# A convolution stem's backward pass: input gradient on plane differences, whose planes are turned to be the weight gradient's operands

## The chip, the cores and the metric

The kernel runs on one core of a Trainium2 chip. Its engines are TensorE (PE, matrix products into PSUM; PEld is its loading of weights), VectorE (DVE), ScalarE (ACT), GpSimd (POOL) and SyncE (SP, which here issues nearly all DMA transfers). Each runs its own list of instructions in order, and they wait for one another by semaphores. The metric is the device time of one execution in microseconds; lower is better.

## The reference

The forward pass is a convolution over time with 31 taps and stride 2, a normalisation over time of each batch and channel, and a GELU. The kernel returns the forward result and the four gradients.

```python
B, T, D, K = 2, 16000, 256, 31          # x [B,T,D], w [K,D,D], bf16
s = 2
L = (T - K) // s + 1                    # 7985
h = sum(einsum('blc,cd->bld', x[:, i:i + s * L:s, :], w[i]) for i in range(K))
mu, var = mean and variance of h over l
h = (h - mu) / sqrt(var + 1e-5) * gn_gamma + gn_beta
out_0 = gelu(h)
out_1, out_2, out_3, out_4 = gradients of x, w, gn_gamma, gn_beta for grad_out
```

## The kernel before

**The arithmetic.** A convolution by 31 taps is cut by the residue of time into sub-convolutions, and two of them are computed with three products instead of four (sums of data planes against differences of weights, or the other way round). This is done twice, which gives nine combinations of a branch `br` and a leaf `lf`, each one of A, B_, C_; the leaf B_ is shared, and its product is added to those of A and C_ as a "seed". Where a third such split is made, a leaf's 16 matmuls of G (`g_leaf`) become 4 (`g_outer`, or `g_three_b` for leaf B_) plus 8 (`g_three_ac`), and the seed has one more term. In the kernel before, leaf B_ is split everywhere, leaf A in the second batch (the set `GO`), and leaf C_ nowhere in G (`GOC` is empty).

**Stages.** F0 and F1 are the forward convolution of the two batches, each in four chunks (`forward`, `f_sums` for the sums of planes on DVE, `f_mm` L596 for the matmuls, `f_seed`); the GELU and its derivative of batch 0 (`gelu_batch`, `gelu_unit`, L954 to L980, one channel half `dh` of 1024 columns at a time) run on ACT and DVE beside F1. G0 and G1 are the input gradient (`input_grad`): for each batch, chunk `c`, half `pr` and branch, matmuls through `g_mm` (L1162). Its data are the planes of the gradient at h, which `e_load` and `e_comp` make from stored tensors and which `g_sums` (L1121) adds up: `first` for the branches, `second` for leaves A and C_, `third` for the further split. `g_seed` (L676 to L687) puts the shared product into the PSUM banks of A and C_, with `g_three_b`'s, `g_outer`'s and leaf B_'s kept results (`GRB`); `g_evac` (L691) takes finished banks out. The GELU of batch 1 runs beside G0. W is the weight gradient (`weight_grad`, matmuls at L1447): nine combinations n, each with sums of x (`w_add` L1413, `pair_x` L1508) and differences of the gradient at h (`leaf_d` L1587, `pair_d` L1516).

**What joins G and W.** W needs time on the partitions, so the gradient at h is turned by DMA (`dn_turn`: two turns of 512 KB and two stores for each chunk) and stored in time order in `dn_d`. `d2_piece` reads it back in seven pieces for each batch, subtracts on DVE (L1357) and stores the operands of eight of the nine combinations in `d2_d`; `d_tile` loads them in W. G itself works on sums of planes with differences of weights, so that none of its own planes is an operand of W.

**Order.** A recording class `Plan` holds every operation with its duration, and orders them by due times: those of PE from their place in the list, the others backwards from who needs them, shifted by a table `lead` for each kind of operation and stage. Per engine, the written order is the order of issue. SP has one list for all loads, stores and turns; a turn is `dma_start_transpose` (L420), another transfer L415. PSUM is four tiles `ring` of two banks; a branch takes two (`px`, `pt`), and two branches are in work at once.

Of the kernel before, what the change touches and what calls it, by code (L numbers as in the profile page):

```python
# [10 lines left out]
FP32 = mybir.dt.float32  # L11
# [27 lines left out]
class Plan:  # L39
# [3 lines left out]
    def __init__(self, tc):  # L43
# [10 lines left out]
            "F0 f_mm f_three_ac": -2.5,  # L54
            "F0 f_mm f_three_b": -4.0,
            "F0 f_mm pe_turn": 9.5,
            "F0 f_three_b f_first": 2.0,
            "F0 f_three_b forward": 2.5,
            "F0 keep f_first": 4.5,
            "F0 load load_w": -4.5,  # L60
            "F0 put x_first": -4.5,
            "F0 tt second": -1.0,
            "F0 tt third": -1.5,
            "F0 turn w2_part": 8.0,
            "F0 turn x_load": -3.5,
            "F0 ve f_first": -1.0,
            "F0 ve f_seed": -4.0,
            "F0 w_sub f_first": 2.0,
            "F1 f_mm f_leaf": -4.0,
            "F1 f_mm f_three_ac": -3.0,  # L70
            "F1 f_mm f_three_b": -9.5,
            "F1 f_three_b forward": 4.5,
            "F1 gelu_unit gelu_batch": 3.0,
            "F1 load gelu_unit": -2.0,
            "F1 tiny elem_finalize": 2.0,
            "F1 tiny fwd_stats": -11.5,
            "F1 tt f_sums": 1.5,
            "F1 tt gelu_unit": -4.0,
            "F1 tt second": -7.5,
            "F1 turn x_load": -3.0,  # L80
            "G0 e_comp conv_stem_kernel": -1.0,
            "G0 g_mm g_three_ac": 3.0,
            "G0 g_mm g_three_b": -3.0,
            "G0 g_three_b input_grad": 6.0,
            "G0 keep g_evac": -3.0,
            "G0 load dn_turn": 1.0,
            "G0 load e_load": 4.5,
            "G0 load gelu_unit": 2.0,
            "G0 load load_w2": 4.0,
            "G0 tiny elem_finalize": -8.5,  # L90
            "G0 tt first": -2.0,
            "G0 tt second": -9.0,
            "G0 turn gelu_batch": -7.0,
            "G0 w_sub load_w2": -8.0,
            "G1 e_comp conv_stem_kernel": 12.5,
            "G1 g_mm g_leaf": -4.0,
            "G1 g_mm g_outer": -1.5,
            "G1 g_mm g_three_ac": -4.0,
            "G1 keep g_evac": -10.5,
            "G1 load dn_turn": -11.5,  # L100
            "G1 load e_load": -2.5,
            "G1 load g_evac": 20.0,
            "G1 signed g_seed": -7.5,
            "G1 spread e_comp": -5.5,
            "G1 sub d2_piece": -7.5,
            "G1 tt first": 9.5,
            "G1 tt second": -5.5,
            "G1 tt third": -2.0,
            "G1 ve_neg g_seed": 11.5,
            "W keep w_keep": -2.0,  # L110
            "W keep weight_grad": 3.0,
            "W leaf_d weight_grad": -2.0,
            "W pair_x weight_grad": -1.5,
            "W turn out0_late": -7.0,
            "W ve w_done": 12.0,
            "W ve weight_grad": -3.5,
            "W w_add weight_grad": -2.0,
            "W w_add x_tile": 3.0,
            "W w_both weight_grad": 9.0,
            "W w_emit w_done": 7.5,  # L120
            "W w_mm w_leaf": -3.5,
            "W w_mm w_single": 0.5,
            "W w_pairs weight_grad": -2.5,
        }
        self.room, self.mixed = 2048.0, 2.2
        self.overlap = {"DVE": 0.084, "ACT": 0.1}
        self.npe = 0
        self.stage = "F0"

# [205 lines left out]
def conv_stem_kernel(  # L335
# [217 lines left out]
    def i_tap(q, par, br, lf):  # L553
        return 8 * q + par + 4 * (lf == C_) + 2 * (br == C_)
# [1204 lines left out]
```

## Time and profile before

| | |
|---|---|
| runs | 1185.14, 1185.56, 1185.71 us; median 1185.56 |
| span of the profiled execution (the page has no other time of it) | 1187.8 us |
| forward matmuls (L596), first and last start | 4.7 and 428.8 us |
| matmuls of the input gradient (L1162) | 416.3 and 861.0 us |
| matmuls of the weight gradient (L1447) | 861.2 and 1183.5 us |
| DMA traffic | 255.17 MB in 334100 packets |

A group of instructions is shown as line, engine, operation, out<-in and shapes, count, then busy time and the mean duration of one, then the idle time of the engine just before them and who ended it. Matmuls overlap in the pipeline, so that their mean duration is a latency; what one costs is the busy time of the group divided by its count. Some matmul records are missing from a trace; weight loads tell the true count, one for each matmul. The rows themselves stand in the prediction.

### The profile page before, as it was taken

What the parts mean: (1) busy time and instruction counts of PE and PEld (TensorE: products, weight loads), DVE (VectorE), ACT (ScalarE), POOL (GpSimd) and SP (SyncE); (2) the same over time, 40 slices, a digit from 0 to 9 for tenths busy, and PEclk for the clock granted to TensorE, in tenths of its full rate; (3) what the DMA queues carried; (4) which work ended last, traced back from release to release, by engine and by line L of the source; (5) the groups of instructions that cost most, each with busy time, mean ns of one, the idle gap of its engine ahead of it and who ended that gap; (6) DMA issues with size and microseconds to landing.
All of it is one profiled execution on the core that took longest, in us unless ns stands there. A gap on an engine that the chain in (4) does not pass through costs nothing.

```text
span 1187.8 us, 19338 instructions
## 1 busy us (share of the span) xinstructions
PE 1149.0 (97%) x7739; PEld 763.5 (64%) x7796; DVE 1047.6 (88%) x1358; ACT 570.0 (48%) x873; POOL 18.9 (2%) x67
## 2 busy tenths in 40 slices
PE   5999999999999999999999999999999999989998
PEld 3888889777777964444444444444488656656685
DVE  7997898799999989999879997788889898777995
ACT  1254454788885578978884476433322212111200
POOL 0000000000000000000000000000000000000000
PEclk9999999999999999999999999999999999999999
DMA  9446949968986799567639998697998824986774
GB/s 212 73 115 122 200 121 182 205 146 204 204 209 124 270 353 252 167 225 186 221 115 292 270 329 265 161 318 266 317 235 266 271 90 151 359 300 198 239 219 140
DMA packets 334100, 255.17 MB, mean 215 GB/s; under 512 B 187500, under 2 KB 312682, under 8 KB 325738
## 3 DMA queue, kind: packets, MB, share of 16 engines
q1 hardware_dynamic: 333818, 253.93, 76.6%
q8 instruction: 61, 1.00, 0.3%
q14 instruction: 29, 0.24, 0.1%
q0 software_dynamic: 192, 0.00, 0.0%
HBM read 118.95 MB, written 89.62 MB: 176 GB/s over the span
## 4 chain that ended last, share of the span: by engine, by line
PE 46%; DVE 14%; DMA 6%; issue 4%; ACT 1%; SPq 0%; DVEq 0%; ACTq 0%
PE ps L1162 27%; PE ps L1447 15%; PE ps L596 4%; DVE arena L1413 3%; DMA arena<-in_x_dram 2%; DMA arena<-dnd 2%; DVE arena L1357 2%; DVE arena L1587 2%; DVE ps L676 1%; DVE arena L676 1%; DVE arena L1516 1%; DVE arena L1508 1%; DMA dnd<-arena 1%; DVE arena L1121 1%; DVE ps L1540 1%
## 5 line engine op out<-in xcount | busy, mean ns | idle before, releaser
L1162 PE MATMUL ps<-arena 128*128 128x512 bf16 x1974 | 429.7, 376 | 6.6 <-DVE ps L676 3.6
L596 PE MATMUL ps<-arena 128*128 128x256 bf16 (+4 forms) x3460 | 408.2, 281 | 17.8 <-DVE arena L551 7.1
L596 PEld LDWEIGHTS <-arena 128*128 128x128 bf16 x3460 | 338.1, 99 | 87.7 <-DVE arena L551 7.5
L1162 PEld LDWEIGHTS <-arena 128*128 128x128 bf16 x2016 | 197.3, 98 | 237.7 <-issue 6.8
L1447 PE MATMUL ps<-arena 128*128 128x256 bf16 (+1 forms) x2305 | 312.1, 298 | 10.5 <-DVE arena L1508 7.3
L1447 PEld LDWEIGHTS <-arena 128*128 128x128 bf16 x2320 | 228.1, 98 | 94.6 <-DVE arena L1508 8.7
L691 ACT ACTIVATE arena<-ps 128x1024 f32<-128x1024 f32 (+1 forms) x143 | 145.7, 1020 | 285.3 <-PE ps L1447 98.1
L561 DVE TENSOR_TENSOR arena<-arena 128x1087 bf16<-128x1087 bf16 (+3 forms) x211 | 175.5, 866 | 13.7 <-PE ps L596 12.4
L968 DVE TENSOR_TENSOR arena<-arena 128x1024 bf16<-128x1024 bf16 x160 | 107.0, 683 | 8.5 <-ACT arena L962 3.9
L1413 DVE TENSOR_TENSOR arena<-arena 128x4096 bf16<-128x4096 bf16 x38 | 86.3, 2284 | 20.8 <-DMA arena<-in_x_dram 19.5
L1121 DVE TENSOR_TENSOR arena<-arena 128x516 bf16<-128x516 bf16 (+3 forms) x176 | 83.6, 506 | 8.6 <-PE ps L1162 8.0
L676 DVE TENSOR_TENSOR ps<-ps,arena 128x1024 f32<-128x1024 f32 x60 | 73.1, 1224 | 7.9 <-PE ps L1447 4.5
L1357 DVE TENSOR_TENSOR arena<-arena 128x768 bf16<-128x768 bf16 (+3 forms) x112 | 65.4, 636 | 9.9 <-DMA arena<-dnd 4.7
L711 ACT ACTIVATE arena<-ps 128x512 bf16<-128x512 f32 (+1 forms) x64 | 36.9, 578 | 70.4 <-PE ps L596 67.9
L676 DVE TENSOR_TENSOR ps<-arena,ps 128x1024 f32<-128x1024 f32 x44 | 53.8, 1223 | 9.3 <-PE ps L1162 5.5
L1532 ACT COPY ps<-ps 128x256 f32<-128x256 f32 x54 | 19.3, 357 | 78.7 <-PE ps L1447 77.6
L1587 DVE TENSOR_TENSOR arena<-arena 128x2304 bf16<-128x2304 bf16 x36 | 47.4, 1348 | 4.8 <-PE ps L1447 4.8
L1516 DVE TENSOR_TENSOR arena<-arena 128x1024 bf16<-128x1024 bf16 x76 | 48.7, 682 | 1.6 <-DMA arena<-d2d 1.6
L551 DVE TENSOR_TENSOR arena<-arena 128x2048 bf16<-128x2048 bf16 (+1 forms) x52 | 49.8, 989 | 0.0
L958 DVE SCALAR_TENSOR_TENSOR arena<-arena 128x1024 bf16<-128x1024 bf16 x32 | 39.0, 1219 | 11.3 <-ACT arena L956 11.1
L1189 ACT ACTIVATE ps<-ps 128x512 f32<-128x512 f32 x48 | 27.9, 582 | 41.1 <-PE ps L1162 38.0
L1508 DVE TENSOR_TENSOR arena<-arena 128x2048 bf16<-128x2048 bf16 x38 | 45.3, 1216 | 1.2 <-PE ps L1162 1.2
(79 smaller groups left out, 632.8 us busy)
## 6 DMA issues: line engine op xcount, KB each, us to landing
arena<-in_x_dram SPq DMA_DIRECT2D x40, 1024.0 KB, 9.8
arena<-d2d SPq DMA_DIRECT2D x16, 1216.0 KB, 11.5
out_dram<-arena SPq DMA_DIRECT2D x14, 1024.0 KB, 4.4
d2d<-arena SPq DMA_DIRECT2D x30, 384.0 KB, 7.1
arena<-dnd SPq DMA_DIRECT2D x10, 960.0 KB, 5.8
vl<-arena SPq DMA_DIRECT2D x36, 256.0 KB, 3.3
arena<-vl SPq DMA_DIRECT2D x9, 1024.0 KB, 6.8
hd<-arena SPq DMA_DIRECT2D x8, 1024.0 KB, 5.0
```

Source lines behind the costliest of these rows:

```text
L561: lambda: nc.vector.tensor_tensor(out=o, in0=a, in1=b, op=ALU.add))
L596: yield nc.tensor.matmul(ps[:, dh, cs], lhsT=wt, rhs=mv, start=s0, stop=False, skip_group_check=True)
L676: add("DVE", dve(1024, 1), [out], [a, b], lambda: nc.vector.tensor_tensor(out=out, in0=a, in1=b, op=op))
L691: lambda: nc.scalar.activation(out=out, in_=ps, func=ACT.Copy, scale=scale))
L968: add("DVE", dve(1024), [o], [a, b_], lambda: V.tensor_tensor(out=o, in0=a, in1=b_, op=op))
L1121: lambda: nc.vector.tensor_tensor(out=o, in0=a, in1=b, op=ALU.add))
L1162: yield nc.tensor.matmul(ps[:, e, 0:wide], lhsT=lt, rhs=mv, start=s0, stop=False, skip_group_check=True)
L1357: lambda: nc.vector.tensor_tensor(out=out, in0=a, in1=b_, op=ALU.subtract))
L1413: add("DVE", dve(4096), [o], [a, b], lambda: nc.vector.tensor_tensor(out=o, in0=a, in1=b, op=ALU.add))
L1447: yield nc.tensor.matmul(ps[:, s, c0:c1], lhsT=lt, rhs=mv, start=s0, stop=False, skip_group_check=True)
L1516: add("DVE", dve(1024), [d4[:, j]], [d], lambda j=j, o=o, st_=st_: nc.vector.tensor_tensor(out=d4[:, j], in0=d[:, o:o + 3 * st_ + 1:st_, : ...
L1587: add("DVE", dve(2304), [DL[i3, b]], [D2[b]], lambda b=b, i3=i3, o_=o_: nc.vector.tensor_tensor(out=DL[i3, b], in0=D2[b][:, o_:o_ + 17:2, ...
```

## The change

1. G works on differences of planes with sums of weights (`g_sums` subtracts, `w2_part`, `load_w2` and `w2_outer` add). Its planes are then W's operands: `dl_turn` turns the nine planes of each chunk, 64 KB at a time, and stores them in `dl_d`, from which `d_tile` loads. `dn_turn`, `d2_piece` and their DRAM tensors go. The turns of a chunk are listed behind branch B_ of its second half, into a ring of four buffers `DNO`.
2. Two sums that differ by a shift become one instruction with an access pattern of one dimension more (`third`, `later`), which writes both. The forward's sums also cover fewer columns. `g_seed` and `f_seed` handle both halves, or both leaves, in one instruction; all of G's seeds are plain sums now.
3. Leaf C_ is split for all of the second batch (`GOC`).
4. `gelu_unit` handles both channel halves at once, W's `pair_x`, `pair_d` and `leaf_d` both batches.
5. The gradient at h is loaded by channel half (`e_load`, `e_comp`), in two pairs of buffers for the first batch's four chunks and one pair after; PSUM is one tile; some buffers of W lie elsewhere; the planner gets new leads, finer ones for each chunk or combination (`fine`), and less spare time for `dl_turn`.

```diff
-    dn_d = [dram.tile([NDR, D], BF16, name=f"dnd{b}") for b in range(NB)]
-    d2_d = [dram.tile([9, P, 19 * D], BF16, name=f"d2d{b}") for b in range(NB)]
+    dl_d = [[dram.tile([NDL, D], BF16, name=f"dld{b}_{i}") for i in range(9)] for b in range(NB)]
...
+        def part(v, n, ks=None):
+            ks = ks or [list(d) for d in v.ap[1:-1]]
+            return bass.AP(tensor=v.tensor, offset=v.offset + lo, ap=[list(v.ap[0]), *ks, [XM, 4], [1, n]])
...
         def third(lf, u):
             o = ops[lf]
-            tt(u[0], o[:, 0], o[:, 1], behind)
-            tt(u[1][:, 0:F - 1], o[:, 1, 0:F - 1], o[:, 0, 1:F], behind)
+            tt(part(u, n), part(o[:, 0], n, [[1, 2]]), part(o[:, 1], n, [[0, 2]]), behind)
...
     def e_load(b, c):
-        for t, d in ((EG, dy_d[b][c]), (EH, h_d[b][c])):
-            load(t.rearrange("p d e k f -> p (d e k f)"), d[:], 1 << 20, 4096, "SP")
+        for dh in range(2):
+            for t, d in zip(EGH[dh if 4 * b + c < 4 else 0], (dy_d[b][c], h_d[b][c])):
+                load(t.rearrange("p e k f -> p (e k f)"), d[:, 2048 * dh:2048 * dh + 2048], 1 << 19, 4096, "SP")
+            e_comp(b, c, dh)
...
-    def dn_turn(b, c, o):
-        for dh in range(2):
-            turn(o.rearrange("p r a d -> p (r a) d")[:, :, dh * P:(dh + 1) * P],
-                 EG[:, dh].rearrange("p e k f -> p (e k f)"), 524288)
...
+    def dl_turn(b, c, planes):
+
+        for br in (ORDER if (b, c) != (1, 3) else (C_, B_, A)):
+            for lf in (C_, A, B_):
+                ds = DNO[4 * b + c < 3]
+                o = ds[tbc[0] % len(ds)]
+                tbc[0] += 1
+                pl = planes(br, lf)
+                for dh in range(2):
+                    for j in range(2):
+                        turn(o[:, :, j, dh * P:(dh + 1) * P], pl[j][:, dh, 0:256], 65536)
+                t = dl_d[b][3 * MIR[br] + MIR[lf]][:]
+                dst = bass.AP(tensor=t.tensor, offset=t.offset + ((48 if b else 0) + 512 * c) * D,
+                              ap=[[2 * D, P], [256 * D, 2], [1, 2 * D]])
+                load(dst, o.rearrange("p m j d -> p m (j d)"), 262144, 1024, "POOL")
...
-                lambda: nc.vector.tensor_tensor(out=o, in0=a, in1=b, op=ALU.add))
+                lambda: nc.vector.tensor_tensor(out=o, in0=a, in1=b, op=ALU.subtract))
...
         def third(br, lf=B_):
-            tt(u[:, 0, :, 0:n], e[:, :, 0, 0:n], e[:, :, 1, 0:n])
-            tt(u[:, 1, :, 0:n - 1], e[:, :, 1, 0:n - 1], e[:, :, 0, 1:n])
+            x, y = e[:, :, 0, 0:n], e[:, :, 1, 0:n]
+            ends = bass.AP(tensor=x.tensor, offset=x.offset, ap=[list(x.ap[0]), list(x.ap[1]), [1, 2], [1, n]])
+            mid = bass.AP(tensor=y.tensor, offset=y.offset, ap=[list(y.ap[0]), list(y.ap[1]), [0, 2], [1, n]])
+            tt(u.rearrange("p e d f -> p d e f")[:, :, :, 0:n], ends, mid)
...
     def g_seed(br, px, pt, outer, both):
-            ve(vt, ts, vx, ALU.subtract)
-            if both and br == A:
-                for e in range(2):
-                    half(px[:, e], px[:, e], tc_[e], ALU.add)
...
+        if both:
+            p = twice(pt[:], True)
+            if br == B_:
+                spread(GTB, p, 2)
+            else:
+                plus(GTB, p, GRB, [GTB], [pt[:], GRB])
+            o, i = both_ways()
+            plus(o, i, GTB.rearrange("p k e f -> p k (e f)"), [pt[:], px[:]], [px[:], GTB])
...
-    GOC = set()
+    GOC = {(1, c, pr) for c in range(NCK) for pr in range(2)}
...
-    def d2_piece(b, pc):
...
     def pair_x(p, x):
-        x4 = p[0]
-        add("DVE", dve(2048), [x4], [x], lambda: nc.vector.tensor_tensor(
-            out=x4, in0=x[:, 0:8:2, :], in1=x[:, 1:8:2, :], op=ALU.add))
+        o = both(p[0][0], p[1][0], [[1, 2048]])
+        i = [both(x[0][:, j], x[1][:, j], [[1024, 4], [1, 512]]) for j in range(2)]
+        add("DVE", dve(4096), [o], i, lambda: nc.vector.tensor_tensor(out=o.rearrange("p b (f c) -> p b f c", c=512),
+                                                                      in0=i[0], in1=i[1], op=ALU.add))
...
     for b, c, pr, br, planes in input_grad():
...
-        if br == B_ and (b, c, pr) in D2AT:
-            plan.hold = plan.npe
-            for pc in D2AT[b, c, pr]:
-                d2_piece(0, pc)
-            plan.hold = -1
-        if (b, c, pr, br) == (1, 0, 1, A) and GOC:
+        if (pr, br) == (1, B_):
+            dl_turn(b, c, planes)
+        if (b, c, pr, br) == (0, 3, 1, A) and GOC:
             w2_outer(C_)
-        if (b, c, pr, br) == (1, 2, 1, B_):
-            for pc in range(7):
-                d2_piece(1, pc)
```

More of the change, by code (lines that the diff above doesn't have):

```diff
@@ L93, in __init__ @@
[L93 to L105, printed above, removed]
@@ new lines, in __init__ @@
+            "G0 tiny elem_finalize": -9.5,
+            "G0 tt first": -60.0,
+            "G0 tt gelu_unit": -0.5,
+            "G0 tt second": 1.0,
+            "G0 turn dl_turn": 1.0,
+            "G0 turn gelu_batch": -8.5,
+            "G0 zero e_comp": 7.5,
+            "G1 e_comp e_load": 13.0,
+            "G1 g_mm g_leaf": -1.0,
+            "G1 g_mm g_outer": -6.0,
+            "G1 g_mm g_three_ac": -8.0,
+            "G1 g_mm g_three_b": -3.5,
+            "G1 keep g_evac": 4.5,
+            "G1 load dl_turn": 11.0,
@@ L1558, in place @@
         def place(n):
-            ks = ("all",) + (("early",) if n < 2 else ()) + (("late",) if n not in (3, 5) else ())
+            ks = (("all",) if n else ()) + (("early",) if n < 2 else ()) + (("late",) if n not in (3, 5) else ())
             turn_[0] += 1
```

650 lines of the change are left out of this document (364 added, 286 removed).

## The prediction

> **What bounds the kernel now.** I read the busy times of the engines first, then the same by stage, then who ended TensorE's waits.
>
> ```profile
> span 1187.8 us, 19338 instructions
> PE 1149.0 (97%) x7739; PEld 763.5 (64%) x7796; DVE 1047.6 (88%) x1358; ACT 570.0 (48%) x873; POOL 18.9 (2%) x67
> ```
>
> ```profile
> 0.00:40.00 40.00, 27.05 (x207) 20.57 (x208) 32.89 (x43) 7.16 (x13) 1.55 (x9) 0.96 0.72 158
> 40.00:416.00 376.00, 371.20 (x3160) 308.31 (x3159) 346.20 (x463) 227.96 (x423) 5.61 (x13) 1.00 0.76 172
> 416.00:640.00 224.00, 222.84 (x1085) 108.22 (x1106) 202.38 (x318) 178.05 (x224) 6.75 (x25) 1.00 0.73 218
> 640.00:861.00 221.00, 215.59 (x987) 98.36 (x1006) 189.26 (x298) 101.78 (x124) 4.42 (x19) 1.00 0.90 281
> 861.00:1188.00 327.00, 312.28 (x2307) 228.09 (x2320) 276.89 (x240) 55.02 (x89) 0.53 (x1) 0.99 0.74 224
> ```
>
> ```profile
> PE ps L1447 <- DVE arena L1508: 7.3, 5, 4.2
> PE ps L596 <- DVE arena L551: 7.1, 2, 4.0
> PE ps L596 <- DMA arena<-in_x_dram: 5.8, 2, 4.7
> PE ps L1162 <- DVE ps L676: 3.6, 5, 1.3
> ```
>
> ```profile
> L1447 PE MATMUL ps<-arena x2305: 269/273/418, 861.2 to 1183.5; 128*128 128x256 bf16 x152, 128*128 128x512 bf16 x41
> ```
>
> The second fence is busy time by stretch: bounds and length, then PE, PEld, DVE, ACT and POOL (with counts), the granted TensorE clock, DMA share and GB/s. The stretches are the start, the rest of the forward, input gradient G in two parts (its b=0 gelu part and the rest), and weight gradient W. The reader is to see that TensorE sets the time in every stage: it is idle for 1187.8 - 1149.0 = 38.8 us, of which 13.0 lie in the first 40 us, 4.8 in the forward, 1.2 and 5.4 in G, and 14.7 in W, about 4 of these behind the last matmul (last row: first and last start). The clock is full outside the first row. The third fence (waits: total, times, longest) says that what is left is mostly DVE: no single wait is worth more than 7.3 us. So matmul work that goes is worth its full price, and DVE work that goes is worth only part of 38.8 us.
>
> **TensorE: leaf C of the second batch.** Today each of its (chunk, half, branch) iterations multiplies leaf C by 16 matmuls 512 wide (g_leaf: 2 results x 4 shifts x 2 halves of the channels). Split, it is g_outer's 4 plus g_three_ac's 8, as leaf A of that batch already is. That is 4 fewer in 4 chunks x 2 halves x 3 branches = 24 iterations: 96 matmuls.
>
> ```profile
> L1162 PE MATMUL ps<-arena 128*128 128x512 bf16 x1974 | 429.7, 376 | 6.6 <-DVE ps L676 3.6
> L1162 PEld LDWEIGHTS <-arena 128*128 128x128 bf16 x2016 | 197.3, 98 | 237.7 <-issue 6.8
> ```
>
> Each matmul has one weight load, so 2016 ran and 42 records are missing; 429.7 / 2016 = 0.213 us each (the row's mean of 376 ns is overlapped latency, not a price). 96 x 0.213 = **-20.5 us**. Nothing else changes the count of matmuls. The price is bounded below by 0 only if G stops being TensorE's; that is a rival.
>
> **VectorE.** The terms come from these groups (count | busy us, mean ns).
>
> ```profile
> L1357 DVE TENSOR_TENSOR arena<-arena 128x768 bf16<-128x768 bf16 (+3 forms) x112 | 65.4, 636 | 9.9 <-DMA arena<-dnd 4.7
> L1121 DVE TENSOR_TENSOR arena<-arena 128x516 bf16<-128x516 bf16 (+3 forms) x176 | 83.6, 506 | 8.6 <-PE ps L1162 8.0
> L561 DVE TENSOR_TENSOR arena<-arena 128x1087 bf16<-128x1087 bf16 (+3 forms) x211 | 175.5, 866 | 13.7 <-PE ps L596 12.4
> ```
>
> ```profile
> L561 DVE TENSOR_TENSOR arena<-arena 128x1088 bf16<-128x1088 bf16 x87 | 61.8, 717 | 7.9 <-PE ps L596 7.1 <-ACT arena L511 0.7
> L561 DVE TENSOR_TENSOR arena<-arena 128x2176 bf16<-128x2176 bf16 x31 | 39.8, 1283 | 0.2
> L1121 DVE TENSOR_TENSOR arena<-arena 128x514 bf16<-128x514 bf16 x68 | 28.1, 422 | 0.9 <-PE ps L1162 0.9
> L1121 DVE TENSOR_TENSOR arena<-arena 128x516 bf16<-128x516 bf16 x68 | 27.6, 419 | 5.6 <-PE ps L1162 5.5
> L1121 DVE TENSOR_TENSOR arena<-arena 128x1036 bf16<-128x1036 bf16 x32 | 22.1, 690 | 2.1 <-PE ps L1162 1.6
> L1121 DVE TENSOR_TENSOR arena<-arena 128x2072 bf16<-128x2072 bf16 x8 | 9.8, 1229 | 0.0
> L968 DVE TENSOR_TENSOR arena<-arena 128x1024 bf16<-128x1024 bf16 x160 | 107.0, 683 | 8.5 <-ACT arena L962 3.9 <-ACT arena L960 3.6
> L676 DVE TENSOR_TENSOR ps<-ps,arena 128x1024 f32<-128x1024 f32 x60 | 73.1, 1224 | 7.9 <-PE ps L1447 4.5 <-ACT arena L691 3.4
> L683 DVE TENSOR_TENSOR arena<-ps,arena 128x512 f32<-128x512 f32 x16 | 10.9, 683 | 1.8 <-ACT arena L691 1.6
> L1508 DVE TENSOR_TENSOR arena<-arena 128x2048 bf16<-128x2048 bf16 x38 | 45.3, 1216 | 1.2 <-PE ps L1162 1.2
> ```
>
> From 717 ns (1088) and 1283 ns (2176) a bf16 sum costs 151 ns plus 0.520 ns per element; from 683 and 1224 ns an fp32 one costs 142 ns plus 1.057 ns.
> - The 112 differences of d2_piece go: -65.4.
> - The plane sums become 80 of 1032 elements (0.69 each), 32 of 1036 and 8 of 2072: 55.2 + 22.1 + 9.8 = 87.1, so +3.5 although 12 sums for leaf C are new.
> - The forward's 211 become 126 shorter and joined ones (35 of 2080 elements, 35 of 2064, the rest of 936 to 4192): 158.7 by the line above, so -16.8.
> - G's seeds: 72 of 1024 fp32 and 32 of 512 (88.1 + 21.9 = 110.0) become 56 of 2048 at 2.31: 129, so +19.
> - Gelu joined over both channel halves: 80 of 2048 or 1856 elements replace 160 (109 to 95), the cubic's 16 replace 32; about -17.
> - W's 150 twin instructions become 75: at 0.15 us each -11, of which records that overlap hide some; I take -6. Three sums of weights for leaf C: 3 x 1.22 = +3.6.
>
> Together -79 us, DVE about 968. None of it is on the path except where TensorE waits for DVE (the 20 us above). I take -3 us from DVE: -1 in the start (its sums are 4% to 6% shorter), -1 in the forward, -3 in W, and +2 in G for the longer seeds below. The bounds: -12 (all but the start and tail idle nearly halved) and +16 (the second rival).
>
> An unknown here is the rate of the joined sums, which read a shift by one element and a step of zero in one instruction. The nearest rows: 514 elements with one operand at an odd element took 422 ns, 516 without took 419. So the odd start is free, and I take the full rate; the step of zero in a middle dimension no row shows. Were all joined sums half as fast, 1032 more elements' time in each of 80 would add 80 x 0.54 = 43 us in G and some 50 in the forward: DVE would be back near 1060, today's load, and the -3 would be 0. The Trainium skill (VectorE: DVE Perf Modes, Mode 2×_1P) asks for 4-byte alignment for two 16-bit results per cycle, which speaks against these sums; by it they would be the half-rate ones and the sum 1165 instead of 1162. The trace disagrees for an odd start (422 against 419 ns).
>
> **The planes' way to the weight gradient.** Out go 16 turns of 512 KB, 16 stores of 512 KB, 14 reads back (12.1 MB) and 70 stores of pieces (19 MB), 47 MB in all. In come 288 turns of 64 KB and 72 stores of 256 KB, 36 MB (sizes from the code).
>
> ```profile
> DMA packets 104842, 110.87 MB, mean 249 GB/s; under 512 B 49171, under 2 KB 92163, under 8 KB 100099
> ```
>
> That is all of G's traffic. The DMA engines were 0.73 and 0.90 busy in G; with a quarter of 111 MB gone, less matmul time to hide it in, but more 256-byte packets, I expect about the same share and no term. The issue queue is the doubt:
>
> ```profile
> L420 SPq DMA_TRANSPOSE arena<-arena x8: 1231/1246/1481, 236.2 to 299.9; - x8
> L420 SPq DMA_TRANSPOSE arena<-arena x15: 1872/2532/5757, 446.8 to 743.4; - x15
> L420 SPq DMA_TRANSPOSE arena<-in_grad_out_dram x8: 1560/2628/11997, 429.9 to 604.0; - x8
> L420 SPq DMA_TRANSPOSE arena<-in_w_dram x4: 1266/1283/2553, 192.7 to 198.0; - x4
> L420 SPq DMA_TRANSPOSE arena<-arena x1: 2087/2087/2087, 715.3 to 715.3; - x1
> L415 SPq DMA_DIRECT2D d2d<-arena x70: 359/379/2963, 637.2 to 843.3; - x70
> L415 SPq DMA_DIRECT2D arena<-hd x23: 319/366/881, 415.7 to 729.2; - x23
> ```
>
> These are times that SP itself is held (ns, min/median/max). The first row is turns of 256 KB in the forward, the second those of 512 KB in G (and the one of 32 KB). Their minima give 1.231 - 192 KB x 0.641/256 = 0.75 us for 64 KB. Bounds: in proportion to bytes 0.31; and the fifth row, the single 32 KB turn, held SP 2.09 us, in a crowded stretch. The fourth row's 1266 is a 128 KB turn beside 256 KB ones, as long as they. I take 0.75, on the line through the rows from uncrowded time. A chunk of the second batch then costs SP 36 x 0.75 + 9 stores x 0.40 + 4 half loads x 0.37 + 2 output stores x 0.36 = 33 us, hidden behind 216 x 0.213 = 46.0 us of its matmuls. What queues behind the turns on SP are the loads of h and dy for the next chunk (e_load); in the second batch both channel halves now pass through one buffer, so they follow each other.
>
> ```profile
> arena<-hd SPq DMA_DIRECT2D x8, 1024.0 KB, 7.8
> L1067 ACT ACTIVATE arena<-arena,stats 128x1024 bf16<-128x1024 bf16 x8 | 9.3, 1230 | 2.1 <-DMA d2d<-arena 1.4 <-DMA arena<-hd 0.7
> L1081 ACT COPY arena<-arena 128x768 bf16<-128x768 bf16 (+1 forms) x48 | 34.8, 757 | 5.9 <-DVE arena L1071 4.3 <-POOL arena L1098 0.7 <-POOL arena L424 0.7
> ```
>
> A half takes at most the 7.8 of today's 1 MB load, then 4 x 1.23 + 1.2 + 4 x 0.76 = 9.2 of affine steps, one sum and spreads; two take 34 us of the 46. If SP is late, g_sums and TensorE are late next.
>
> **Seeds.** Joined, A's sum waits for both leaves of branch B to be evacuated, where its first half waited for one only. Behind B's last leaf stand: evacuation 1.5, sum 2.3, the wait for g_three_ac, second sum 2.3, in all some 7.7 us. In the built order 40 matmuls (8.5 us) stand between on TensorE. Covered by 0.8 us, so a plane sum of DVE (0.69 to 1.23) in between can stall it: the +2 above.
>
> **Sum.** The span of the profiled run is 1187.8, 0.2% over the median of 1185.56; the page has no other time for it. 1187.8 - 20.5 - 3 = 1164.3 of span, and 2.2 less for a timed run: **1162 us**.
>
> **Rivals.**
> 1. *SP is full* (slower). Place: G. If a turn of 64 KB holds SP for the 1.23 us of a 256 KB one, a chunk of the second batch needs 36 x 1.23 + 5.8 = 50 us against 46: 16 late over four. In the first batch 4 x 50 plus some 33 for the gelu (8 x 2.63 for its turns, 24 loads and stores of about 0.4, 2 of weights) stand against 225 - 28 (no plane is ready in the first half chunk): 36 late. Of 52, some 16 may lag into W, whose first combination needs one plane. 1162 + 36 = 1198. It decides from (46.0 - 5.8)/36 = 1.1 us per turn, and the gain is gone at about 1.2. For it: the 128 KB and 32 KB turns. Against: both fell into crowded stretches. The Trainium skill (DMA: Bandwidth & Descriptors, Measured) says that transfers under 64 KB are "descriptor-dominated" and asks for larger ones; no run here shows such turns in number.
> 2. *The joined seeds cost their latency*: 2 us in each of the 8 halves of the second batch if the cover of 8.5 us is broken by plane sums every time: +16, 1178. For: DVE L676 already ends the waits of G. Against: 5 waits in 445 us.
> 3. *DVE's relief closes the idle*: W's 10 and G's 6 us shrink to 4: 1150.
> 4. *The change does not do what it says*: the matmuls go, but G stays as long because loads, not TensorE, pace it (DMA share 0.90): 1185.
>
> **How the numbers follow.** Forecast (1155 to 1172) 0.47; rival 1 0.20; rival 2 0.15; rival 3 0.12; rival 4 0.06. A range of 8 in 10 leaves out rival 1: 1150 to 1187. This kernel's runs differ by 0.05%, so 0.2% (2.4 us) tells a change from none. Faster: 0.47 + 0.15 + 0.12 = 0.74 and part of rival 4, 0.76; same 0.04; slower 0.20.
>
> **What would show it.** The 512-wide matmuls of G down by 96 and G about 20 us shorter show the first term; a group of 288 turns with a median under 0.9 us on SP kills rival 1, over 1.1 us with TensorE waiting for plane sums or loads proves it. DVE near 968 shows the second part; a joined 1032-element sum at 0.69 us and not 1.22 the rate. TensorE's waits for the seeds' line above 15 us would be rival 2. I am wrong if G is not shorter.

## The result, and the profile after

The changed kernel takes **1336.38 us** (median of 4 runs, 1328.71 to 1340.41) against 1185.63 for the kernel before beside it (1185.14 to 1186.7): ratio 1.126, 95% interval 1.123 to 1.129. The forecast was 1162, its range 1150 to 1187. The profiled execution took 1334.03 us. Ratios below are to the kernel before, timed beside each run; where a run's time is given without one, the kernel ran once.

First the busy times of the page, then busy time by stretch of the changed kernel (bounds, length, PE, PEld, DVE, ACT, POOL with counts, granted TensorE clock, DMA share, GB/s). The stretches are the forward, the first batch's input gradient G in three pieces, the second batch's, and the weight gradient W.

```profile
span 1332.3 us, 18807 instructions
PE 1163.7 (87%) x7646; PEld 760.9 (57%) x7700; DVE 983.5 (74%) x856; ACT 568.3 (43%) x849; POOL 22.8 (2%) x79
```

```profile
0.00:412.80 412.80, 400.08 (x3405) 332.34 (x3406) 358.72 (x349) 232.51 (x422) 8.32 (x30) 1.00 0.72 170
412.80:640.00 227.20, 172.08 (x762) 78.43 (x776) 149.75 (x163) 144.82 (x182) 8.64 (x23) 0.91 0.69 198
640.00:726.00 86.00, 48.52 (x196) 20.96 (x199) 35.72 (x49) 22.15 (x30) 0.39 (x4) 0.78 0.53 149
726.00:764.00 38.00, 31.04 (x130) 13.39 (x131) 20.80 (x23) 19.46 (x25) 1.86 (x5) 0.91 0.51 138
764.00:996.40 232.40, 198.77 (x854) 87.73 (x871) 134.82 (x102) 94.37 (x105) 3.02 (x16) 0.93 0.51 145
996.40:1332.30 335.90, 313.19 (x2309) 228.07 (x2321) 283.71 (x173) 55.00 (x89) 0.53 (x1) 0.98 0.72 228
```

The same stretches of the kernel before, with the batches apart:

```profile
0.00:414.60 414.60, 396.85 (x3351) 327.50 (x3352) 377.69 (x503) 233.84 (x434) 7.15 (x22) 1.00 0.75 170
414.60:648.40 233.80, 232.59 (x1137) 113.43 (x1159) 212.18 (x337) 182.02 (x231) 6.75 (x25) 1.00 0.74 223
648.40:861.00 212.60, 207.24 (x949) 94.53 (x967) 180.86 (x281) 99.09 (x120) 4.42 (x19) 1.00 0.89 278
861.00:1187.80 326.80, 312.28 (x2307) 228.09 (x2320) 276.89 (x240) 55.02 (x89) 0.53 (x1) 0.99 0.74 224
```

The loss is in G: 583.6 us (412.8 to 996.4) against 446.4, most of it in the first batch, 351.2 against 233.8. The forward is 1.8 us shorter, W 9.1 longer. In the worst piece, 640 to 726 us, no compute engine is over 0.57 busy, and the DMA engines are at 0.53: the bound is none of the rows in this view. It is the engine that issues the transfers. Here is how long SP itself was held by turns (L542) and by other transfers (L537), in ns, min/median/max:

```profile
L542 SPq DMA_TRANSPOSE arena<-arena x305: 1167/1244/4231, 233.0 to 978.1; - x153
L542 SPq DMA_TRANSPOSE arena<-in_grad_out_dram x16: 1593/2566/12543, 210.2 to 645.8; - x16
L537 SPq DMA_DIRECT2D dld<-arena x72: 359/512/1930, 469.9 to 980.6; - x72
L537 SPq DMA_DIRECT2D arena<-hd x32: 319/557/1532, 214.0 to 853.4; - x32
L537 SPq DMA_DIRECT2D arena<-dyd x16: 320/498/1669, 389.0 to 865.4; - x16
```

The first row holds 288 turns of 64 KB, one of 32 KB and 16 of 256 KB, and its median is 1.244 us. Adding up the durations of all 450 turns and transfers that SP issued during G gives 511 us, of 583.7 between G's first and last weight load: 380 of turns, 36 of the 8 turns of grad_out, 95 of the other 153. In the kernel before it is 187 us of 446. The timeline of SP, in a stretch of the second batch (start, duration, what):

```profile
849.18 4.09 SPq L542 DMA_TRANSPOSE arena<-arena  x3
853.37 0.52 SPq L537 DMA_DIRECT2D arena<-hd  x1
854.01 0.37 SPq L537 DMA_DIRECT2D dld<-arena  x1
854.43 10.26 SPq L542 DMA_TRANSPOSE arena<-arena  x8
864.74 0.58 SPq L537 DMA_DIRECT2D dld<-arena  x1
865.42 0.41 SPq L537 DMA_DIRECT2D arena<-dyd  x1
865.93 0.92 SPq L537 DMA_DIRECT2D dld<-arena  x2
866.90 4.53 SPq L542 DMA_TRANSPOSE arena<-arena  x3
```

SP goes from one instruction to the next with pauses of at most 0.12 us. The load of h, at 853.4, and that of dy for the same half, at 865.4, stand twelve microseconds apart because eight turns are listed between them. Who waits for that, in the view of waits during G (total, times, longest):

```profile
ACT arena L826 <- DMA out_dram<-arena: 38.9, 4, 14.2
ACT arena L1098 <- DMA dyd<-arena: 29.6, 6, 8.6
DVE arena L1201 <- DMA arena<-hd: 26.7, 3, 19.8
ACT arena L1210 <- DMA arena<-dyd: 17.9, 4, 6.1
DVE arena L1272 <- DMA arena<-arena: 15.0, 2, 10.7
```

Evictions wait until an output store has left its buffer, the gelu for its own store, the affine steps on h and dy for their loads, plane sums until a turn has read the old plane. These stores and loads stand among the turns in SP's list. TensorE in turn waits for the engines that wait: in G for evictions (L826), for ACT's copies in PSUM (L1344) and for the seeds on DVE (L1384).

```profile
PE ps L1317 <- ACT arena L826: 45.0, 14, 7.5
PE ps L1317 <- ACT ps L1344: 44.4, 14, 9.9
PE ps L1317 <- DVE ps L1384: 38.8, 9, 23.1
```

### The profile page after: what moved, and what is told of

It reads as the page before. It is cut to its first block, busy times and chain, and to the rows that moved or that the text cites. A ratio compares the mean times of both kernels' runs of the same rounds, so it can differ in the third digit from the quotient of the medians.

```text
span 1332.3 us, 18807 instructions
## 1 busy us (share of the span) xinstructions
PE 1163.7 (87%) x7646; PEld 760.9 (57%) x7700; DVE 983.5 (74%) x856; ACT 568.3 (43%) x849; POOL 22.8 (2%) x79
## 4 chain that ended last, share of the span: by engine, by line
PE 27%; SPq 17%; DMA 9%; DVE 5%; ACT 3%; issue 3%; POOL 0%; DVEq 0%; ACTq 0%
PE ps L1549 20%; SPq L542 14%; PE ps L1317 7%; SPq L537 3%; DMA arena<-dyd 2%; DMA arena<-in_x_dram 2%; DVE arena L1272 1%; DMA out_dram<-arena 1%; ACT arena L826 1%; DMA arena<-dld 1%; DVE arena L1623 1%; DVE arena L1518 1%; DMA yd<-arena 1%; DMA arena<-arena 1%; DMA arena<-hd 1%
## 5 line engine op out<-in xcount | busy, mean ns | idle before, releaser
L1317 PE MATMUL ps<-arena 128*128 128x512 bf16 (+1 forms) x1880 | 445.8, 396 | 133.2 <-ACT arena L826 45.0
L826 ACT ACTIVATE arena<-ps 128x1024 f32<-128x1024 f32 (+1 forms) x143 | 144.5, 1019 | 311.7 <-PE ps L1549 99.3
L689 DVE TENSOR_TENSOR arena<-arena 128x2064 bf16<-128x2064 bf16 (+7 forms) x126 | 156.9, 1267 | 22.3 <-PE ps L731 21.6
L1272 DVE TENSOR_TENSOR arena<-arena 128x1032 bf16<-128x1032 bf16 (+2 forms) x120 | 84.5, 730 | 56.5 <-PE ps L1317 40.9
L1106 DVE TENSOR_TENSOR arena<-arena 128x2048 bf16<-128x2048 bf16 (+1 forms) x80 | 95.7, 1196 | 38.5 <-ACT arena L1098 33.0
L1384 DVE TENSOR_TENSOR ps<-ps,arena 128x2048 f32<-128x2048 f32 x40 | 91.7, 2296 | 36.9 <-PE ps L1317 25.9
L1518 DVE TENSOR_TENSOR arena<-arena 128x4096 bf16<-128x4096 bf16 x38 | 86.0, 2286 | 9.5 <-DMA arena<-in_x_dram 7.8
L1091 ACT ACTIVATE arena<-arena,stats 128x1024 bf16<-128x1024 bf16 (+1 forms) x32 | 37.5, 1211 | 40.1 <-issue 14.8
L1221 ACT COPY arena<-arena 128x768 bf16<-128x768 bf16 (+1 forms) x64 | 36.0, 615 | 42.3 <-DVE arena L1212 42.1
L1614 DVE TENSOR_TENSOR arena<-arena 128x4096 bf16<-128x4096 bf16 x19 | 43.3, 2288 | 12.5 <-DMA arena<-in_x_dram 12.2
L1384 DVE TENSOR_TENSOR arena<-ps,arena 128x2048 f32<-128x2048 f32 x16 | 36.6, 2290 | 20.3 <-ACT arena L826 14.8
L1697 DVE TENSOR_TENSOR arena<-arena 128x4608 bf16<-128x4608 bf16 x18 | 45.7, 2551 | 1.3 <-DMA arena<-dld 1.3
```

The lines of the kernel that those rows point to most:

```text
L689: lambda: nc.vector.tensor_tensor(out=o, in0=a, in1=b, op=ALU.add))
L826: lambda: nc.scalar.activation(out=out, in_=ps, func=ACT.Copy, scale=scale))
L1106: add("DVE", dve(nf), [o], [a, b_], lambda: V.tensor_tensor(out=o, in0=a, in1=b_, op=op))
L1272: lambda: nc.vector.tensor_tensor(out=o, in0=a, in1=b, op=ALU.subtract))
L1317: yield nc.tensor.matmul(ps[:, e, 0:wide], lhsT=lt, rhs=mv, start=s0, stop=False, skip_group_check=True)
L1384: lambda: nc.vector.tensor_tensor(out=o, in0=a, in1=b, op=ALU.add))
```

## The experiments

Theory S: a turn holds SP for a fixed 1.24 us, and SP's in-order list became G's bound. Rival D: the bytes on the transposing path set the time. Rival P: the turns keep the planes, and the next chunk's sums wait for them.

**The turns themselves.** Four kernels change only `dl_turn`. In `t256`, shown here, a copy makes the plane contiguous, so that one turn takes it; in `const_src` the turns read `zt2[:]`, a tile of zeros, in place of the plane; in `no_turns` the inner loops go, in `half_turns` those of the second `dh`. In t256 the four buffers `DNO` are two for copies and two for what was turned.

```diff
-                for dh in range(2):
-                    for j in range(2):
-                        turn(o[:, :, j, dh * P:(dh + 1) * P], pl[j][:, dh, 0:256], 65536)
...
+                k = ds[2 + tbc[0] % 2].rearrange("p m j d -> p (m j d)")
+                for j in range(2):
+                    add("DVE", dve(512, 4), [k], [pl[j]], lambda k=k, q=pl[j], j=j: nc.vector.tensor_copy(
+                        out=k.rearrange("p (m j h f) -> p j h m f", m=2, j=2, h=2)[:, j],
+                        in_=q[:, :, 0:256].rearrange("p h (m f) -> p h m f", m=2)))
+                turn(o.rearrange("p m j (h d) -> p (m j h) d", h=2), k.rearrange("p (g f) -> p g f", f=128), 262144)
```

> The changed kernel with the same 18.9 MB turned by 72 turns of 256 KB and not 288 of 64 KB: VectorE first copies a plane's two parts and channel halves into one contiguous buffer (144 copies of 512 elements, an estimated 0.2 to 0.35 us each, 30 to 50 us of VectorE, from the 0.69 us that 2048 elements of tensor_scalar took), and the ring of four buffers is shared, two for copies and two for what was turned. Theory S (a turn holds SyncE for a fixed 1.24 us, and SyncE's list is full): 216 turns fewer free 270 us of SyncE's 519 in the input gradient, which is TensorE's again; 1160 to 1185. Rival D (the bytes that are transposed set the time): nothing changes, 1310 to 1345. Rival P (the planes are held by turns that have not read them, and the next chunk's sums wait): also fast here, since a copy frees a plane, 1160 to 1190.

> The changed kernel, but all 288 turns read one constant tile that nobody writes, and not the planes (what the weight gradient then multiplies is this constant). Turns, their sizes, their buffers and stores stay. Theory S: SyncE is held as before, 288 times 1.24 us; only its waits for planes go: 1270 to 1340. Rival P (planes held until they are turned): the planes are free at once, 1160 to 1200. Rival D: 1310 to 1345.

> The changed kernel without the 288 turns; the 72 stores stay and store what the buffers held (the weight gradient's operands are not the planes). If the turns are the whole loss, by S, P or D: 1155 to 1175, input gradient 415 to 430 us. If another part of the change costs something (joined seeds, one load buffer, loads by halves), it stays: 1185 or more.

> The changed kernel with 144 of the 288 turns (those of one channel half; the other half of the buffers is stored as it was, so that part of the weight gradient's operands is not computed). Theory S: SyncE's work in the input gradient falls from 519 to about 338 us, below TensorE's 409; nearly all of the loss is gone, 1160 to 1195. Rival D (bytes): half of the loss stays, about 1245. Rival P: in between, 1180 to 1250.

Measured: t256 1292.41 (ratio 1.090, 1.088 to 1.092), const_src 1339.46, no_turns 1195.7, half_turns 1220.05. With no plane held and none waited for, const_src is as slow as the changed kernel, and its turns hold SP as long (median 1244 ns): rival P falls. Against no_turns, half the turns cost 24 us and the other half 116: not the proportion that D asks for, but what a queue would show that has room until it is full; the two kernels differ in order too. The forecasts of S missed all the same: t256 by over 100 us, half_turns by 25, and no_turns is 20 above its range. In t256 G begins at 443.8 us and not at 412.8, because the planner made another order, and DVE waited for its copies' buffers (view of waits, t256):

```profile
DVE arena L1260 <- DMA arena<-arena: 24.0, 8, 8.5
```

**Copies on GpSimd; fewer transfers on SP; two other parts of the change.** `t256_pool` moves the copies, `pool_stores` takes G out of the stages whose transfers all go to SP (`ONE`), `nt_gelu_half` undoes the gelu's joining of channel halves, `nt_goc_off` sets `GOC = set()`; the last two on top of no_turns.

> As t256 (72 turns of 256 KB from a contiguous copy), but GpSimd makes the copies, so that VectorE never waits for a copy buffer that a turn has not read yet. In t256 VectorE waited 24.0 us for DMA arena<-arena at the copies, the gelu of the second batch came late by it, and the two halves of chunk (0,3) and (1,0) beside it took 45.6 and 58.6 us. Theory S (SyncE's list alone was the loss, and t256's rest was VectorE's wait for copies): 1195 to 1230, that is no_turns (1195.7) and a little. Rival D' (a turn costs by its bytes somewhere else than on SyncE): stays at 1280 or more. Rival: GpSimd's copies are slow (over 1.3 us each) or hold VectorE: 1240 to 1300.

> The changed kernel with its 288 turns of 64 KB, but all transfers of the input gradient that the code writes for GpSimd (72 stores of turned planes, 16 gelu stores, 16 output stores, 24 of weights) are issued by GpSimd and not by SyncE: some 104 x 0.55 = 57 us and more fall off SyncE's list. Theory S: SyncE had 519 us of work in the 582 of the input gradient, so it shortens by 50 to 80 us: 1255 to 1290. Theory P (waits for planes): no change, 1320 to 1345.

> no_turns (the 288 turns left out, the weight gradient's operands are not the planes) with the gelu's sums, products and sigmoids again by channel half (1024 elements for each instruction) and not by both at once (2048). In no_turns (1195.7) the eight halves of the first batch took 249.7 us against 234.2 before; its TensorE stood still 15 times for 0.3 to 3.3 us (15.9 us), mostly until an ACT copy or eviction. Theory G (instructions of 2048 elements, 2.0 to 2.3 us long, stand in the way of the copies and evictions that TensorE waits for): the first batch falls by 8 to 15 us, 1181 to 1189. Rival J (the joined seeds of 2.29 us do it): no change, 1194 to 1198.

> no_turns with leaf C unsplit again in the second batch (GOC empty): 96 matmuls more, seeds of 1024 elements for branch A and C as for the unsplit leaf. The term of the prediction, 96 x 0.213 = 20.5 us: 1214 to 1218. Rival (the split gives less, since seeds and evictions stand on the path): 1196 to 1210.

Measured: t256_pool 1301.45 (1.097, 1.094 to 1.100; again G begins late, at 443.3), pool_stores 1273.64 (1.074, 1.071 to 1.077), nt_gelu_half 1214.16, nt_goc_off 1231.45. t256_pool came out where rival D' had put it, 70 us above S's range. pool_stores gave the 60 us that S asked for, with all 288 turns in place: SP's sum fell from 511 to 440 us and G by 68. That speaks for SP's list and against a cost of the turns elsewhere, though here too the order is new. nt_goc_off lost 36 in all, outside both its forecasts. In its second batch TensorE was busy for 19.9 us more than in no_turns (206.3 against 186.5), the price of 96 matmuls; the stretch is 16 us longer, and W, in a new order, 25. nt_gelu_half's forward ended 14 us later, so it tells nothing of the gelu. The lesson was one of method: a planner that orders by due times answers each edit with a new order, worth tens of microseconds.

**The order kept.** From here the turns stay in the plan with their old durations, and only what is emitted at their place changes; every other instruction keeps its place on its engine.

```diff
-    def turn(out, in_, nbytes, slack=None):
+    def turn(out, in_, nbytes, slack=None, go=None):
...
-            lambda: nc.sync.dma_start_transpose(out=out, in_=in_), ...
+            go or (lambda: nc.sync.dma_start_transpose(out=out, in_=in_)), ...
```

> The changed kernel without the 288 turns (the weight gradient's operands are not the planes), but with the order of every other instruction on every engine kept as the changed kernel has it; in no_turns the planner had made a new order. Theory S: 1190 to 1200, as no_turns. Rival O (the order itself, made by the planner with cheap turns in its sums, costs): 1210 or more.

> The changed kernel in its own order, but each plane's four turns of 64 KB are one turn of 256 KB, at the place of the first (it takes 1024 columns that lie side by side, gap and all, so that the weight gradient's operands are not the right ones). 72 turns, the same 18.9 MB, no copies. Theory S: SyncE's work falls by 216 x 1.26 = 272 us; 1190 to 1215. Rival D (bytes on the way of the transposes): 1310 or more. In t256 and t256_pool copies and a new order were mixed in; the input gradient began 30 us later there.

> The changed kernel in its own order, each of the 288 turns a plain transfer of the same 64 KB from the same plane to the same buffer, not turned (the weight gradient's operands are not the right ones). Number, bytes and waits as in the changed kernel; only what holds SyncE differs: 0.35 to 0.60 us by the plain transfers of the trace, against 1.24. Theory S: SyncE's work falls by some 200 us below TensorE's: 1190 to 1230. Rivals D and P: 1310 or more.

> The kernel before with leaf C split in three half chunks of the second batch, (1,1) both halves and (1,2) the first, where its buffers are free between the pieces for the weight gradient: 3 x 3 x 4 = 36 matmuls fewer, 36 x 0.213 = 7.7 us, against three sums of weights and 3 sums of planes for each of two chunks on VectorE, which is 0.86 busy there. If TensorE's price holds: 1177 to 1181. Rival: VectorE and the pieces' buffers take it back: 1184 to 1192.

Measured: kept_none 1175.02 (0.990, 0.988 to 0.992), kept_wide 1184.63 (0.997, 0.995 to 0.999), kept_plain 1199.49, before_goc 1230.63 (1.036, 1.034 to 1.038). The rows of SP for the 72 wide turns of kept_wide, then for the 288 plain transfers of kept_plain:

```profile
L1260 SPq DMA_TRANSPOSE arena<-arena x72: 1232/1336/4179, 444.1 to 813.2; - x72
```

```profile
L1259 SPq DMA_DIRECT2D arena<-arena x288: 593/619/2944, 444.7 to 832.7; - x144
```

A turn of four times the bytes holds SP nearly as long as one of 64 KB (1.34 against 1.24 us); over kept_none, the same bytes in a quarter of the turns cost 10 us and not 161; the same number, bytes and waits as plain transfers 24. D falls; S stands. kept_none and kept_wide came out below S's ranges. SP's sum of durations during G against G's length:

| kernel | SP held in G, us | G, us | time, us |
|---|---|---|---|
| kept_none | 134 | 427.5 | 1175.0 |
| kept_wide | 252 | 433.7 | 1184.6 |
| kept_plain | 324 | 446.9 | 1199.5 |
| no_turns (own order) | 129 | 442.2 | 1195.7 |
| half_turns (own order) | 327 | 463.4 | 1220.1 |
| pool_stores (own order) | 440 | 515.2 | 1273.6 |
| const_src (own order) | 501 | 585.4 | 1339.5 |
| the changed kernel | 511 | 583.7 | 1336.4 |
| t256, with copies (own order) | 228 | 504.4 | 1292.4 |
| t256_pool, with copies (own order) | 227 | 510.0 | 1301.5 |
| copy_pool (below), with copies | 184 | 458.6 | 1208.0 |
| copy_mixed (below), with copies | 209 | 474.7 | 1220.5 |
| copy_sp (below), with copies | 224 | 487.8 | 1234.0 |

In the order kept, from 134 to 324 us, the first 190 of SP cost G 19, a tenth each; from 440 to 511 each costs about one, by two runs that differ in order. The five kernels with copies show that SP's sum is not all: with no more than 228 us of SP their G is 459 to 510 us, and what makes them longer than kept_wide is what else they change: the copies with their two buffers, and in t256 and t256_pool the order. before_goc, whole, lost where it should have won: two of its half chunks took 52.8 and 38.9 us instead of 27, in a new order again, so it does not price the split.

**What is left without turns, and a whole version.**

> kept_none (1175.0), but the weight gradient's first combination reads for the second batch the first batch's tile of operands, which was stored long before, and not the one whose last rows are stored at the end of the input gradient (so the weight gradient is not right). In kept_none TensorE waited 7.6 us for DMA arena<-dld at that place, and that stage was 335.0 us against 327.0 before. Theory W (the handover by store and load is what the change adds there): 1165 to 1169. Rival: another wait takes its place (sums of x): 1172 to 1176.

> kept_none (1175.0), with the first batch's joined seeds (2048 elements, both leaves in one instruction, 2.29 us) as two instructions of 1024 right behind one another, leaf A's first. The first batch's input gradient took 239.1 us against 234.2 before. Theory J (the joined seed is late by its second half): 1170 to 1173. Rival (the wait is for the ACT copies beside them, or DVE is later by the second instruction's start): 1174 to 1177.

> The changed kernel in its own order, whole and right, with 72 turns of 256 KB: at the place of a plane's first turn VectorE makes the contiguous copy (2 x 0.289 us as in t256, 41 us for all) and SyncE issues one turn; a store that would be overtaken in the now two output buffers goes out ahead of that turn. kept_wide, the same without copies and with wrong columns, took 1184.6. Theory S: 1185 to 1200. Rival V (VectorE waits for copy buffers as in t256, 24 us, and the gelu gets late by it): 1205 to 1260.

> copy_sp with the 72 stores of turned planes issued by GpSimd, not by SyncE: some 40 us less on SyncE's list, of which it has room by then, and no waiting for a turn's end in that list. Theory S: 1178 to 1192, 3 to 10 us under copy_sp, as kept_none is 10 under kept_wide. Rival: GpSimd's own small copies for the gradient's edges wait behind the stores: as copy_sp or more.

> The changed kernel in its own order, whole, with 72 turns of 256 KB. In copy_pool (1208.0, VectorE copies, GpSimd stores) the first batch's input gradient took 263.8 us and the second's 193.6, against 245.3 and 187.2 in kept_wide (1184.6): VectorE, 0.86 busy in the first batch without copies, has no room for 21 us more. Here GpSimd makes the first batch's copies and SyncE its stores; VectorE copies and GpSimd stores in the second. The buffers are given out as the turns are issued (copy_sp and copy_pool gave them out by the planes' numbers, and their turns are not issued in that order, so planes were lost). Theory S and V (SyncE, then VectorE's room): 1186 to 1196, 0 to 1% over the kernel before. Rival: GpSimd's copies (0.925 us each) hold the small copies of the gradient's edges that e_comp needs: 1200 to 1230.

> kept_none (1175.0) with the first batch's joined seeds as two instructions of 1024 elements one behind the other, everything else in place. In kn_seed_apart the new instruction fell under another entry of the table of leads, so that the order changed with it, and it took 1184.6. Theory J (the joined seed is late by its second half, 5.0 us of TensorE's waits): 1170 to 1173. Rival (the waits are not for the second half): 1174 to 1177.

Measured: kn_early_load 1177.26 (0.991, 0.989 to 0.994), kn_seed_apart 1184.64 (0.998, 0.996 to 1.000), copy_sp 1233.98 (1.041, 1.037 to 1.044), copy_pool 1208.01 (1.018, 1.016 to 1.021), copy_mixed 1220.51 (1.028, 1.025 to 1.031), kn_seed_split 1179.97 (0.994, 0.991 to 0.996). Theory W fell: with nothing to wait for in DRAM, the wait at W's start stayed. The views of waits, kept_none first, then kn_early_load with a piece of its SP timeline:

```profile
PE ps L1549 <- DMA arena<-dld: 7.6, 1, 7.6
```

```profile
PE ps L1553 <- DMA arena<-dld: 7.7, 2, 7.2
```

```profile
824.31 11.73 SPq L537 DMA_DIRECT2D arena<-in_x_dram  x4
836.08 1.79 SPq L537 DMA_DIRECT2D arena<-dld  x2
```

The two loads stand behind four loads of x that take from 824.3 to 836.0 to be issued, two of them waiting for matmuls of G. The chain that ended last, in the same trace, has these main pieces:

```profile
828.61 6.87 PE ps L1317 x32
835.50 0.54 SPq L537
836.08 1.31 SPq L537
837.44 11.76 DMA arena<-dld
849.33 0.80 PE ps L1553 x3
```

The last load of x waits for a matmul until 835.5; the two loads of operands are issued right behind it without a wait of their own, and the second lands 11.8 us later, when G has been over since 841.7. So their place in SP's list holds them. Whether their buffer would have been free earlier was not tried. Joined seeds: with them split and the order kept (kn_seed_split), G took 425.9 us against 427.5, but W was 5 us longer and the whole 5 above kept_none, outside both forecasts. In G they cost at most 2 us; their gain or loss in the whole stays open.

In copy_sp and copy_pool some planes are overwritten before they are stored; instructions and transfers are those of a whole kernel. copy_mixed, which mends that, computes everything and is 116 us faster than the changed kernel, still 2.8% slower than before. Its copies on GpSimd took 1.02 us for 512 elements, against 0.29 on DVE in copy_pool; with two buffers for copies and two for what was turned, they waited another 63.0 us for turns (DVE's copies 31.8 in copy_sp and 16.7 in copy_pool):

```profile
L1277 POOL COPY arena<-arena 128x512 bf16<-128x512 bf16 x72 | 71.1, 1022 | 86.2 <-DMA arena<-arena 63.0 <-DMA hd<-arena 12.8 <-DVE arena L1106 7.8
```

No whole kernel here beats the one before. kept_wide, whose operands are the wrong columns, shows where such a version would lie if contiguous planes were free: 0.3% under it.

## Why the prediction was wrong, step by step

**The step that failed first is a price**: "I take 0.75, on the line through the rows from uncrowded time", for SP's time per turn of 64 KB. It is 1.244 us (median; 1.32 in the mean). The line was drawn through two sizes above the one in question and assumed that SP is held in proportion to the bytes added; between 64 and 256 KB the runs show 1.24 and 1.34 us. The two rows that said so, 128 KB at 1.266 and 32 KB at 2.087, were set aside because "both fell into crowded stretches". The Trainium skill (DMA: Bandwidth & Descriptors, Measured) calls transfers under 64 KB "descriptor-dominated", but it measured the DMA engines' time for loads that GpSimd issues. The cost found here is another one, the time that the issuing SP is held.

**The overlap fell with it**: "hidden behind 216 x 0.213 = 46.0 us of its matmuls". SP's list in G became 511 us long, against 414 of matmuls in kept_none. The price alone does not give the size of the miss. Rival 1 had the mechanism and its place, at a chance of 0.20, but its own sum, 1198, was 138 us short. The test that the prediction named for it, a median over 1.1 us on SP with TensorE waiting, came out at 1.244. It put G's SP time at 4 x 50 + 33 + 4 x 50 = 433 us and 28 before the first plane, 461. Measured are 511 and 72 in which SP issued nothing, 584. Of the 78 us of work, 26 are turns longer than 1.23 (380 against 354), 15 are grad_out's turns (36 against 21), and 37 the other transfers (95 against 58), which took 0.62 us each (95 / 153) and not 0.40. These last two were no effect of the turns: without them, in kept_none, the same instructions held SP for 39 and 93 us. The prediction had put medians where a sum needs means; in the kernel before, 192 such transfers in G had held SP for 111 us, 0.58 each, and the 8 turns of grad_out for 31. The last 44 are pauses, whose cause is shown only in part. SP waited 17 us in G for plane sums (L1272); the rest of its waits was for gelu steps, affine sums, evictions, stores and matmuls. And const_src, where no turn waits for a plane, has 84 us without an issue (585 - 501) against the 72. The rival let SP's surplus spread evenly; the timeline above shows loads that the next planes need behind turns whose results are needed only in W. How much of the miss that order makes was not measured apart.

**TensorE, -20.5**: held in size. There are 1920 weight loads and not 2016; nt_goc_off priced the 96 at 19.9 us; and without turns the second batch fell by 25.4 us, of which 2.5 is idle time of TensorE (5.4 before, 2.8 now) and about 1 the first seven matmuls of W, which lay in that stretch before. kept_none in the same stretches:

```profile
0.00:413.20 413.20, 401.26 (x3405) 333.31 (x3406) 358.72 (x349) 232.50 (x422) 8.36 (x30) 0.99 0.71 170
413.20:652.30 239.10, 229.61 (x1086) 108.16 (x1106) 204.86 (x234) 187.20 (x235) 13.71 (x32) 1.00 0.69 224
652.30:839.50 187.20, 184.37 (x848) 84.55 (x864) 134.97 (x102) 93.36 (x105) 4.21 (x16) 1.00 0.41 134
839.50:1174.50 335.00, 313.82 (x2313) 228.84 (x2326) 283.88 (x174) 56.06 (x90) 0.53 (x1) 0.98 0.72 227
```

Against the kernel before: forward -1.4, first batch +5.3, second -25.4, W +8.2; in all -13.3, where the forecast's terms gave -23.5.

**DVE, -79 to 968 and -3 us of time**: 983.5, so -64; the plane sums, the forward's sums and the seeds came within 3 us each of what was said. The durations of all DVE instructions, added up, fell by 106 us (1139.4 to 1033.7), but they overlapped by 92 us before and by 50 now, so that busy time fell less. Of time, 1.4 of the forward's -2 came; W's -3 became +8.2, of which 7.6 is the wait for its first operands, which no term had. The +2 for longer seeds in G stands against +5.3 in the first batch.

**The rate of the joined sums**: full, as taken. Groups of the changed kernel (count | busy, mean ns):

```profile
L1272 DVE TENSOR_TENSOR arena<-arena 128x1032 bf16<-128x1032 bf16 x80 | 54.2, 693 | 11.6 <-PE ps L1317 11.2
L689 DVE TENSOR_TENSOR arena<-arena 128x2064 bf16<-128x2064 bf16 x35 | 43.0, 1234 | 8.3 <-PE ps L731 8.1
L1384 DVE TENSOR_TENSOR ps<-ps,arena 128x2048 f32<-128x2048 f32 x40 | 91.7, 2296 | 36.9 <-PE ps L1317 25.9 <-ACT arena L1380 6.7 <-ACT arena L826 3.1
```

693 ns for 1032 elements was forecast as 0.69 us, and 2296 for the seeds as 2.31. The Trainium skill (VectorE: DVE Perf Modes, Mode 2×_1P) would have had the joined sums, in which one half of an operand starts at an odd element, at half that rate; the trace disagrees.

**DMA, no term**: the DMA engines did not decide. Their share in G is 0.51 to 0.69, under the 0.74 and 0.89 of before, but with G 137 us longer. In kept_wide, which moves the same bytes in less time, it is 0.94 in the first batch, so that little room is left there:

```profile
413.40:658.70 245.30, 231.46 (x1086) 108.42 (x1106) 204.87 (x234) 186.95 (x235) 10.47 (x32) 0.99 0.94 258
```

The forecast's "a quarter of 111 MB gone" was a slip: by the prediction's own 47 and 36 MB it is a tenth, and G moved 96.9 MB after 110.9. Rivals 2 and 3 did not decide. TensorE waited 38.8 us for the seeds' line, over the 15 that were to mean rival 2, but without turns 5.0: the seeds were late by the turns. And no idle time closed. Rival 4's "loads, not TensorE, pace it" is nearer to what happened than its price, 1185.

## What to carry to other kernels

An issue queue is an engine: price each DMA instruction by what holds the queue, from a row of its own size or as a constant, and not by scaling a larger one's bytes down. Add up the queue's time for each stage, with means and not medians. Here, in a fixed order, a microsecond of it cost the stage a tenth up to 0.73 of the stage (324 of 446.9); between 0.85 and 0.88 it cost about one, as far as two runs tell. When a transfer is cut into smaller ones to spare another engine work, ask what stands behind them in that list and how late it may be.

Where a planner sets the order, take parts away without letting it plan anew: no_turns and kept_none leave out the same turns and differ by 21 us.

## What the runs showed of the hardware

A DMA turn from SBUF to SBUF held SP for 1.24 us at 64 KB and, in kept_wide, for 1.34 at 256 KB (medians; minima 1.167 and 1.232). The one of 64 KB held it as long when it read a constant tile; a plain transfer of the same 64 KB held it for 0.62. The row of 512 KB of the kernel before, with a minimum of 1.87 and a median of 2.53, is the first size here that costs clearly more.

TensorE's granted clock was lower where it idled: 0.78 between 640 and 726 us (0.56 busy), 0.91 to 0.93 in the rest of G, 1.00 in kept_none. The matmuls of G were busy for 450 us in the changed kernel against 414 for the same matmuls in kept_none (sums of the stretches above), so that some of a stall is paid a second time in slower matmuls.
